# Split products with w_out for the last four steps of the first chunk: POOL rounds the blocks, VectorE makes the square

## The chip, the cores and the metric

The kernel runs on one core of a Trainium2 chip. The metric is the device time of one execution in microseconds (us), as a median of runs. The engines are TensorE (PE in the profile; its weight loads are PEld), VectorE (DVE), ScalarE (ACT), GpSimd (POOL) and SyncE (SP, which here only issues transfers). Each engine takes its instructions in the order in which the program gives them to it and waits for the others by semaphores.

## The reference

Block-sparse attention is followed by a two-layer feed-forward block:

```python
# q, k, v: (4, 8, 768, 64); blocks of 32 tokens; mask by blocks
scores = scale * q @ k.T              # where the mask allows
attn = softmax(scores)
x = (attn @ v).transpose(0, 2, 1, 3).reshape(3072, 512)
h = np.maximum(x @ w_in, 0.0)         # w_in: (512, 2048)
return (h * h @ w_out)                # w_out: (2048, 512)
```

A block of queries sees its neighbours, the first and the last block, and three sampled blocks; the first and last block of queries see everything. The weights come as 64-bit floats, the rest as 32-bit floats.

## The kernel before

**Chunks and steps.** The 3072 tokens are worked in eight chunks `c` of 384 tokens (three tiles of 128). The feed-forward block of a chunk, `moe(c)`, has 16 steps `f`, one for each 128 of the 2048 hidden units. `hidden(c, f)` makes 128 hidden units for the 384 tokens: 12 matmuls (L928), four pieces of `w_in` by three products (high x high, low x high, high x low: both `w_in` and `x` are split into a part rounded to the matmul's reduced format, `fp32r`, and a remainder). `finish` (L945) takes the result out of PSUM: relu `r` on ACT, then the square. `project(c, f)` (L965) multiplies the square by block `f` of `w_out` and adds into three PSUM banks, one for each tile of tokens. It runs `LEAD` = 2 steps behind the hidden step, so that `project(c, 14)` and `project(c, 15)` stand at the start of `moe(c + 1)`, after the last hidden step of `c` and before the first of `c + 1`.

**Two ways to project.** In chunk 0, with `PLAIN` = 16, all steps take the plain way: square `gp` in full 32 bits (L952), full `WO[f]`, three matmuls (L972), each of which the hardware runs in two passes. Later chunks take the split way: `gh` rounded by ACT (L955), `gf` in full by DVE (L960), `gl = gf - gh` by POOL (L962), and the block `w_out` as `wo`: a rounded half and a remainder, made by `split` (L887): the rounding on DVE (L892; in chunk 0 on ACT, L890), the subtraction on POOL (L893). A split step has nine matmuls (L982), `gh` by the rounded half, `gh` by the remainder, `gl` by the rounded half for each tile of tokens. The blocks `wi` of `w_in` are made by `split` in the same way, once per step, one step ahead of the hidden step that needs them.

**Unpacking the weights.** In chunk 0 the weights arrive as 64-bit words (`craw`, transfers issued by POOL) and are cut to 32 bits: two operations on ACT (L841, L843) and two on DVE (L852, L853) for a block. The order is the list `cuts`; its last entries are `w_out` 12, `w_in` 15, `w_out` 13, 14 and 15. `cut_next` moves the list on at fixed counts; `need` moves it on where a block is wanted sooner. In the kernel before no call of `need` in the last steps has anything left to do.

**The order of work.** Nothing is rearranged: each engine gets its instructions in the order in which the Python code runs (`manual_schedule`, L1043). `moe` is a generator; after each of its `yield`s a counter `now` goes on by one, and `work.step(now)` adds what the attention of a coming chunk has due then (scores, maxima, exponentials, moves of blocks, products with the values). Around the change the counts are: step 12's project from 78, step 13's from 84, `finish` of step 15 at 89, `moe(1)` from 89 on: the splits of `x` for chunk 1 (`xh` by ACT, L912; `xl` by DVE, L916), attention's maxima (L678 to L682), at 90 the split of `wi` 1, then `project(0, 14)` from 90 and `project(0, 15)` from 93, and the output of chunk 0 at 96. Two lines of `moe` matter most:

```python
            if c == 0 and f > 0:
                split_wo(c, f - 1)          # L1034, before project(c, f - 2)
...
                if c == 1 and f == NF - 1:
                    split_wo(0, f)          # L1018, before project(0, 15)
```

With `PLAIN` = 16 both calls return at once. In iteration `f` of chunk 0 the split of `wi` for step `f + 1` comes first.

**Buffers.** The tiles tagged `w` (raw blocks, `wi`, `wo`, and attention's `pg` and `pgm`) share seven buffers in turn; `gh`, `gf`, `gl` and `r` have two each. Hidden products, scores and attention's outputs share five PSUM banks, the projections have three.

Of the kernel before, what the change touches and what calls it, by code (L numbers as in the profile page):

```python
# [14 lines left out]
AF = mybir.ActivationFunctionType  # L15
ALU = mybir.AluOpType
# [33 lines left out]
TOK = UC * P  # L50
# [45 lines left out]

WO_LOW = 3
W1_LOW = 5
PLAIN = 16


def f32(ap):
# [4 lines left out]
def tile_block_sparse_attention_moe(ctx: ExitStack, tc, kd, knd, qd, qgd, vd, vnd, samp, const, wcat, out):  # L107
# [9 lines left out]
    nc = tc.nc  # L117
# [55 lines left out]
    WO = {f: one.tile([P, DM], F32, name=f"WO{f}") for f in range(WO_LOW)}  # L173
# [637 lines left out]
    wo = {}  # L811
# [3 lines left out]
    acc = {}  # L815
# [67 lines left out]
    def need(f, part):  # L883
        while done["split"] <= cuts.index((f, part)):
            cut_next()

    def split(c, src, name):  # L887
        w = rot.tile([P, 2, DM], F32R, tag="w", name=name, bufs=WBUFS)
        if c == 0:
            nc.scalar.copy(w[:, 0], src)  # L890
        else:
            nc.vector.tensor_copy(w[:, 0], src)  # L892
        nc.gpsimd.tensor_tensor(w[:, 1], src, w[:, 0], op=ALU.subtract)  # L893
        return w

    def split_wo(c, f):
        if c == 0:
            if f < PLAIN:
                return
            need(f, 1)  # L900
        wo[c, f] = split(c, WO[f], f"wo{c}_{f}")

    def parts(c, i, a, z):

# [34 lines left out]
    def hidden(c, f):  # L939
        yield from half_hidden(c, f, 2 if (c, f) in ph else 0, NCC)  # L940
        finish(c, f)
        if f < NF - 1:
            yield 0.7

    def finish(c, f):  # L945
        acc = ph.pop((c, f))
        wi1.pop((c, f), None)
        r = pool["x"].tile([P, TOK], F32, tag="r", name=f"r{c}_{f}", bufs=2)
        nc.scalar.activation(r, acc[:, :TOK], AF.Relu)  # L949
        if c == 0 and f < PLAIN:  # L950
            gt[c, f] = pool["x"].tile([P, TOK], F32, tag="gh", name=f"gp{c}_{f}", bufs=2)
            nc.scalar.activation(gt[c, f], r, AF.Square)  # L952
            return
        gh = pool["x"].tile([P, TOK], F32R, tag="gh", name=f"gh{c}_{f}", bufs=2)
        nc.scalar.activation(gh, r, AF.Square)  # L955
        gf = pool["x"].tile([P, TOK], F32, tag="gf", name=f"gf{c}_{f}", bufs=2)
        if c == 0:
            nc.scalar.activation(gf, r, AF.Square)
        else:
            nc.vector.scalar_tensor_tensor(gf, acc[:, :TOK], 0.0, r, op0=ALU.max, op1=ALU.mult)  # L960
        gl = pool["x"].tile([P, TOK], F32R, tag="gl", name=f"gl{c}_{f}", bufs=2)
        nc.gpsimd.tensor_tensor(gl, gf, gh, op=ALU.subtract)  # L962
        gt[c, f] = (gh, gl)

    def project(c, f):  # L965
        if f == 0:
            acc[c] = [ps_o.tile([P, 512], F32, tag="o", name=f"po{c}_{u}") for u in range(UC)]
        if c == 0 and f < PLAIN:
            need(f, 1)
# [36 lines left out]
    def moe(c):  # L1006
# [6 lines left out]
        if c > 0:  # L1013
            yield 0.7
            if c < NCH:
                wi1[c, 1] = split(c, W1[1], f"wi{c}_1")
            for f in range(NF - LEAD, NF):
                if c == 1 and f == NF - 1:  # L1018
                    split_wo(0, f)
                yield from project(c - 1, f)  # L1020
            emit_out(c - 1)
        if c == NCH:
            return
        for f in range(NF):
            for n in (f, f + 1) if f == 0 else (f + 1,):
                if n < NF and (c, n) not in wi1:
                    if c == 0:
                        need(n, 0)
                    if n in SINGLE:
                        wi1[c, n] = split(c, W1[n], f"wi{c}_{n}")  # L1030
            if c == 0 and f == 0:
                for n in range(2):
                    yield from half_hidden(c, n, 0, NCC // 2)
            if c == 0 and f > 0:  # L1034
                split_wo(c, f - 1)
            if f >= LEAD:
                yield from project(c, f - LEAD)
            if c > 0:
                split_wo(c, f)
            yield from hidden(c, f)  # L1040
# [64 lines left out]
    while work.todo or work.running or now < SPLIT_0[-1]:  # L1105
# [16 lines left out]
        if now in SPLIT_0:  # L1122
            f = 1 + SPLIT_0.index(now)
# [88 lines left out]
```

## Time and profile before

| what | value |
|---|---|
| time, median of 3 runs | 738.68 us (738.59 to 739.42) |
| the profiled execution's own time | 735.78 us |
| its span, first to last instruction | 733.9 us |
| L928, hidden products (960 high, 480 low) | 275.5 and 161.9 us busy |
| L972, plain projections of chunk 0 (96 passes) | 48.6 us busy |
| L982, split projections of chunks 1 to 7 (672 and 336 matmuls) | 211.7 and 134.5 us busy |
| first and last L972 | 55.1 and 151.2 us |
| granted TensorE clock, mean | 0.998 |

The times of the profile count from the first instruction. `busy` is the time in which at least one instruction of a group ran; matmuls overlap, so the start of one to the start of the next tells more than their durations. In a row of the timeline the bracket at the end is the idle time of the engine ahead of it and what ended it. In the windows each engine has its busy time and its number of instructions; behind them come the granted clock, the share of the DMA engines and GB/s.

### The profile page before, as it was taken

To read this page: it belongs to the slowest core of one execution; us is meant where nothing else is said; L and a number is where in the kernel's file an instruction comes from. 1 tells how busy PE (TensorE), PEld (TensorE's weight loads), DVE (VectorE), ACT (ScalarE), POOL (GpSimd) and SP (SyncE) were. 2 spreads that over 40 slices of the span, in tenths; PEclk is the share of its full clock that TensorE was granted. 3 is DMA by queue.
4 is the path that set the end of the run, shared out by engine and by line. 5 is a ranking of instruction groups with operands and counts; after the bars stand their busy time and mean duration, and the time that the engine had idled before them with its cause. 6 is when DMAs were issued, how large, how long until landed. Compare 5 with 4: busy or idle time off the path is not lost.

```text
span 733.9 us, 21489 instructions
## 1 busy us (share of the span) xinstructions
PE 707.5 (96%) x7496; PEld 566.3 (77%) x7496; DVE 530.1 (72%) x1058; ACT 499.7 (68%) x1116; POOL 553.6 (75%) x711
## 2 busy tenths in 40 slices
PE   5879999999999999999999999999999999999997
PEld 3555666677788888877878888887778888888996
DVE  5786888687786868679776877768877686647552
ACT  5877878988856866688775875678776767622222
POOL 8969968368766768869776587768877577868985
PEclk9999999999999999999999999999999999999999
DMA  8978897555545565554635556635455352101001
GB/s 279 228 208 264 241 355 243 146 140 148 169 124 120 168 192 155 125 133 138 186 80 137 166 155 194 152 91 153 119 146 147 97 158 49 34 1 44 1 1 43
DMA packets 91886, 105.10 MB, mean 143 GB/s; under 512 B 13667, under 2 KB 77668, under 8 KB 91780
## 3 DMA queue, kind: packets, MB, share of 16 engines
q1 hardware_dynamic: 85972, 81.15, 41.8%
q0 software_dynamic: 5664, 22.45, 9.1%
q8 instruction: 60, 0.98, 0.6%
q14 instruction: 46, 0.38, 0.2%
q10 hardware_dynamic: 144, 0.13, 0.1%
HBM read 97.39 MB, written 6.29 MB: 141 GB/s over the span
## 4 chain that ended last, share of the span: by engine, by line
PE 82%; DVE 8%; POOL 3%; issue 3%; ACT 3%; DMA 1%; POOLq 0%; DVEq 0%; ACTq 0%
PE ph L928 33%; PE po L982 27%; PE s L478 6%; PE pv L573 6%; PE po L972 5%; PE pvg L734 2%; PE g L664 2%; DVE m L490 1%; PE pt L552 1%; POOL gl L962 1%; DVE p L497 1%; DVE pT L528 1%; DVE gf L960 1%; POOL pgm L700 1%; DVE xl L916 1%
## 5 line engine op out<-in xcount | busy, mean ns | idle before, releaser
L928 PE MATMUL ph<-xh,wi 128*128 128x384 f32 x960 | 275.5, 347 | 0.0
L522 ACT ACTIVATE pm<-p 32x256 f32<-32x256 f32 x528 | 219.2, 415 | 15.2 <-DVE p L497 8.0
L982 PE MATMUL po<-wo,gh 128*128 128x512 f32 x672 | 211.7, 396 | 0.4 <-ACT gh L955 0.3
L893 POOL TENSOR_TENSOR wi<-W,wi 128x512 fp32r<-128x512 f32 x120 | 164.3, 1369 | 60.7 <-DVE wi L892 37.9
L928 PEld LDWEIGHTS ph<-xh,wi 128*128 128x128 f32 x960 | 174.2, 188 | 21.7 <-issue 12.1
L949 ACT ACTIVATE r<-ph 128x384 f32<-128x384 f32 x128 | 63.0, 492 | 173.0 <-PE ph L928 172.4
L893 POOL TENSOR_TENSOR wo<-WO,wo 128x512 fp32r<-128x512 f32 x112 | 144.7, 1292 | 34.5 <-DVE wo L892 33.1
L962 POOL TENSOR_TENSOR gl<-gf,gh 128x384 fp32r<-128x384 f32 x112 | 118.7, 1060 | 65.0 <-DVE gf L960 56.2
L928 PE MATMUL ph<-xl,wi 128*128 128x384 f32 x480 | 161.9, 337 | 0.0
L982 PEld LDWEIGHTS po<-wo,gh 128*128 128x128 f32 x672 | 123.0, 188 | 27.4 <-issue 7.5
L960 DVE SCALAR_TENSOR_TENSOR gf<-ph,r 128x384 f32<-128x384 f32 x112 | 62.0, 554 | 107.7 <-ACT r L949 99.7
L982 PE MATMUL po<-wo,gl 128*128 128x512 f32 x336 | 134.5, 400 | 4.9 <-POOL gl L962 4.8
L928 PEld LDWEIGHTS ph<-xl,wi 128*128 128x128 f32 x480 | 90.2, 188 | 9.1 <-issue 5.4
L892 DVE CAST wo<-WO 128x512 fp32r<-128x512 f32 x112 | 86.4, 772 | 0.0
L982 PEld LDWEIGHTS po<-wo,gl 128*128 128x128 f32 x336 | 63.0, 187 | 24.5 <-POOL gl L962 11.2
L955 ACT ACTIVATE gh<-r 128x384 fp32r<-128x384 f32 x112 | 58.9, 526 | 10.7 <-POOL pgm L700 0.7
L490 DVE TENSOR_REDUCE m<-s 128x2 f32<-128x512 f32 (+1 forms) x96 | 61.0, 675 | 1.6 <-PE s L478 1.5
L892 DVE CAST wi<-W 128x512 fp32r<-128x512 f32 x105 | 60.7, 578 | 0.0
L573 PEld LDWEIGHTS pv<-V,pT 128*32 128x32 f32 x2816 | 42.5, 110 | 23.0 <-issue 13.8
L573 PE MATMUL pv<-V,pT 128*32 128x65 f32 x2816 | 50.8, 222 | 4.9 <-issue 4.0
L478 PE MATMUL s<-KG,q 64*32 64x256 f32 x1408 | 52.9, 382 | 0.0
L972 PE MATMUL po<-WO,gp 128*128 128x512 f32 x96 | 48.6, 622 | 1.9 <-DVE WO L853 1.9
(93 smaller groups left out, 771.6 us busy)
## 6 DMA issues: line engine op xcount, KB each, us to landing
craw<-in_w_dram POOLq DMA_DIRECT2D x32, 512.0 KB, 5.6
V<-in_v_dram SPq DMA_DIRECT2D x462, 32.5 KB, 2.4
KG<-in_k_dram SPq DMA_DIRECT2D x189, 64.0 KB, 1.9
V<-in_v_dram SPq DMA_DIRECT2D x28, 390.0 KB, 5.3
KG<-in_k_dram SPq DMA_DIRECT2D x12, 768.0 KB, 5.8
q<-in_q_dram SPq DMA_DIRECT2D x24, 256.0 KB, 3.1
out_dram<-ot SPq DMA_DIRECT2D x23, 256.0 KB, 4.6
V<-in_v_dram SPq DMA_DIRECT2D x14, 292.5 KB, 5.0
```

What stands on the lines that cost most here:

```text
L478: nc.tensor.matmul(self.sb[e][g * BLK : (g + 1) * BLK, i * NSLOT : (i + 1) * NSLOT], q[r, j, pr, :], kg[r, j, :, pr, :], start=True, stop= ...
L490: nc.vector.tensor_reduce(m[at, e], self.sb[e][at].rearrange("p (i c) -> p i c", i=2), axis=AX, op=ALU.max)
L522: nc.scalar.activation(p[a * BLK : (a + 1) * BLK, g], x[g * BLK : (g + 1) * BLK, :, a], AF.Exp, scale=SCALE)
L573: nc.tensor.matmul(po[h * BLK : (h + 1) * BLK, g * VW : (g + 1) * VW], self.pT[:, g, 2 * e + i, c], v[:, self.u, j, h * VW : (h + 1) * VW] ...
L892: nc.vector.tensor_copy(w[:, 0], src)
L893: nc.gpsimd.tensor_tensor(w[:, 1], src, w[:, 0], op=ALU.subtract)
L928: nc.tensor.matmul(ph[c, f][:, :TOK], wi[:, w, cc], x[:, cc], start=(cc == 0 and i == 0), stop=(cc == NCC - 1 and i == 2),)
L949: nc.scalar.activation(r, acc[:, :TOK], AF.Relu)
L960: nc.vector.scalar_tensor_tensor(gf, acc[:, :TOK], 0.0, r, op0=ALU.max, op1=ALU.mult)
L962: nc.gpsimd.tensor_tensor(gl, gf, gh, op=ALU.subtract)
L972: nc.tensor.matmul(acc[c][u], g[:, u * P : (u + 1) * P], WO[f], start=(f == 0), stop=(f == NF - 1))
L982: nc.tensor.matmul(acc[c][u], g[:, at], w[:, k], start=(f == 0 and i == 0), stop=(f == NF - 1 and i == 2))
```

## The change

The constant `PLAIN` goes from 16 to 12, so steps 12 to 15 of chunk 0 take the split way. For them POOL makes the rounded half of `wo` as well as the remainder, where the code before would have used ACT, and DVE makes the full square `gf`. The rounding of `wi` stays on ACT in chunk 0.

```diff
-PLAIN = 16
+PLAIN = 12
...
-    def split(c, src, name):
+    def split(c, src, name, copy=None):
         w = rot.tile([P, 2, DM], F32R, tag="w", name=name, bufs=WBUFS)
-        if c == 0:
-            nc.scalar.copy(w[:, 0], src)
-        else:
-            nc.vector.tensor_copy(w[:, 0], src)
+        (copy or (nc.vector.tensor_copy if c else nc.scalar.copy))(w[:, 0], src)
         nc.gpsimd.tensor_tensor(w[:, 1], src, w[:, 0], op=ALU.subtract)
         return w
...
-        wo[c, f] = split(c, WO[f], f"wo{c}_{f}")
+        wo[c, f] = split(c, WO[f], f"wo{c}_{f}", None if c else nc.gpsimd.tensor_copy)
...
         gf = pool["x"].tile([P, TOK], F32, tag="gf", name=f"gf{c}_{f}", bufs=2)
-        if c == 0:
-            nc.scalar.activation(gf, r, AF.Square)
-        else:
-            nc.vector.scalar_tensor_tensor(gf, acc[:, :TOK], 0.0, r, op0=ALU.max, op1=ALU.mult)
+        nc.vector.scalar_tensor_tensor(gf, acc[:, :TOK], 0.0, r, op0=ALU.max, op1=ALU.mult)
```

## The prediction

> **What bounds the kernel now.** I read the page's head first, then the chain of waits from 126 to 160 us, then the order of work on POOL, ScalarE (ACT) and VectorE (DVE) in that stretch.
>
> ```profile
> span 733.9 us, 21489 instructions
> PE 707.5 (96%) x7496; PEld 566.3 (77%) x7496; DVE 530.1 (72%) x1058; ACT 499.7 (68%) x1116; POOL 553.6 (75%) x711
> ```
>
> TensorE is busy 96% of the span, so a change matters by what it takes from TensorE's work or adds to its waits. The steps concerned lie here (start, length, what):
>
> ```profile
> 134.00 1.72 PE po L972 x4
> ...
> 137.59 1.40 PE ph L928 x8
> ...
> 140.91 2.57 PE po L972 x6
> 143.48 1.40 PE ph L928 x8
> ...
> 145.69 0.91 PE ph L928 x4
> 146.59 5.15 PE po L972 x12
> 151.74 2.12 PE ph L928 x12
> ...
> 158.34 2.09 PE po L982 x9
> ```
>
> Every piece of this chain is a TensorE piece. L972 is the plain product with `w_out`, six passes a step: step 12 starts at 134.00, step 13 at 140.91, steps 14 and 15 run back to back from 146.59 to 151.74. L982 at 158.34 is a later chunk's step, nine passes. A plain step takes 5.15 / 2 = 2.57 us, a split step 2.09 us.
>
> **What TensorE gains.** Four steps at 2.57 - 2.09 = 0.48 us, so 1.9 us in all, 0.26% of the span. That is all there is to win, and only if the split blocks are there in time.
>
> **What the other engines get.** Nothing changes on ACT: two squares a step become one square for the product (524 ns before, 526 ns after by the same shape), and DVE makes the other. The prices of the rest, each from a row of the same shape (min/median/max ns for L859 and L860, mean ns in the group rows):
>
> ```profile
> L962 POOL TENSOR_TENSOR gl<-gf,gh 128x384 fp32r<-128x384 f32 x112 | 118.7, 1060 | 65.0 <-DVE gf L960 56.2
> L960 DVE SCALAR_TENSOR_TENSOR gf<-ph,r 128x384 f32<-128x384 f32 x112 | 62.0, 554 | 107.7 <-ACT r L949 99.7
> L955 ACT ACTIVATE gh<-r 128x384 fp32r<-128x384 f32 x112 | 58.9, 526 | 10.7 <-POOL pgm L700 0.7
> L859 POOL CAST WI<-ct x1: 746/746/746, 39.1 to 39.1; 128x512 fp32r<-128x512 f32 x1
> L860 POOL TENSOR_TENSOR WI<-ct,WI x1: 1272/1272/1272, 39.9 to 39.9; 128x512 fp32r<-128x512 f32 x1
> L952 ACT ACTIVATE gp<-r x16: 522/524/526, 53.3 to 147.2; 128x384 f32<-128x384 f32 x16
> ```
>
> DVE gets 4 x 0.55 = 2.2 us. POOL gets 4 x (0.75 + 1.27 + 1.06) = 12.3 us. L859 is the very operation that the change puts on POOL, a rounding copy of a 128x512 block. Started one behind the other, rounding and subtraction take 39.9 - 39.1 + 1.27 = 2.07 us. POOL has room for the sum; what decides is where the pieces stand in its order.
>
> ```profile
> 130.83 1.27 POOL L893 TENSOR_TENSOR wi<-W,wi 128x512 fp32r<-128x512 f32 x1 [4.95 <-ACT wi L890]
> 139.04 1.28 POOL L893 TENSOR_TENSOR wi<-W,wi 128x512 fp32r<-128x512 f32 x1 [6.94 <-ACT wi L890]
> 140.26 0.61 POOL L357 COPY KG<-kn 128x512 f32<-128x512 f32 x1
> 140.81 3.01 POOL L700 COPY pgm<-pg 32x192 f32<-32x192 f32 x8
> 152.25 1.30 POOL L893 TENSOR_TENSOR wi<-W,wi 128x512 fp32r<-128x512 f32 x1 [8.43 <-DVE wi L892]
> 153.48 0.62 POOL L357 COPY KG<-kn 128x512 f32<-128x512 f32 x1
> ```
>
> These are the `wi` splits of steps 14 and 15 and of step 1 of the next chunk, each after a long wait (bracket). In `moe`, each new `wo` split stands right behind one of them: wo12 behind wi14, wo13 behind wi15, and wo15 behind wi1 of chunk 1 (wo14 stands alone). POOL takes its instructions in order, so its idle time ahead of these rows cannot be used by the new work behind them.
>
> **wo12, no cost.** wi14 ends at 132.1, so wo12 is complete at 132.1 + 2.07 = 134.2; TensorE wants its second half one pass after 134.00, at 134.23. DVE's new square of step 12 waits for the same relu that ACT makes now. So step 12 saves its 0.48 and TensorE is through with hidden step 14 at 140.91 - 0.48 = 140.43.
>
> **wo13, a short wait.** ACT sets its start:
>
> ```profile
> 134.65 0.49 ACT L949 ACTIVATE r<-ph 128x384 f32<-128x384 f32 x1
> ...
> 138.35 0.62 ACT L890 CAST wi<-W 128x512 fp32r<-128x512 f32 x1
> ...
> 141.86 0.49 ACT L949 ACTIVATE r<-ph 128x384 f32<-128x384 f32 x1
> ...
> 146.63 0.49 ACT L949 ACTIVATE r<-ph 128x384 f32<-128x384 f32 x1 [0.69 <-PE ph L928]
> ...
> 147.58 1.64 ACT L912 CAST xh<-x 128x512 fp32r<-128x512 f32 x3
> ```
>
> The cast of wi15 starts at 138.35 in ACT's order whatever TensorE gains: the relu at 134.65 shows no wait, nor does any ACT row up to 146.63. wi15 leaves POOL at 140.32, wo13 at 140.32 + 2.07 = 142.39. TensorE stands from 140.43, does one pass at about 141.1 (first half), and goes on at 142.45: 142.45 + 8 x 0.232 = 144.31, against 143.48 before. Step 13 is late by 0.8 us net. Behind the DVE square of step 13, which waits for the relu at 134.65, lie the unpacking of the last two `w_out` blocks; they come up to 2 us later and are not wanted before wo14. Hidden step 15 takes its 3.11 us (143.48 to 146.59) and ends at 147.4 instead of 146.59.
>
> **wo14, covered.** After 142.39 POOL has the key copy (0.61), eight moves (3.01), `gl` of step 14 (1.06) and wo14 (2.07). By their place three moves come ahead of wo14: 147.2. With all eight ahead it would be 149.1. TensorE wants it at 147.4; a wait of up to 1.7 us is hidden under the next one. Step 14 then ends at 149.5.
>
> **wo15, the long wait.** It stands behind wi1 of chunk 1, and that waits for a chain that starts when hidden step 15 ends:
>
> ```profile
> 148.22 1.90 DVE L916 TENSOR_TENSOR xl<-x,xh 128x512 fp32r<-128x512 f32 x3 [4.78 <-ACT xh L912]
> 150.03 1.16 DVE L678 TENSOR_REDUCE g<-g 128x1 f32<-128x384 f32 x2
> ...
> 151.66 0.42 DVE L892 CAST wi<-W 128x512 fp32r<-128x512 f32 x1
> ```
>
> Relu at 146.63, square, three roundings of x from 147.58, their remainders on DVE to 150.1, two maxima with small operations, the cast at 151.66, POOL's wi1 at 152.25. So wi1 starts 152.25 - 146.59 = 5.66 us after hidden step 15, and POOL starts its next instruction at 153.48, 6.89 us after. In the kernel before nobody on TensorE's path waits for that: 5.15 us of plain products and then a first hidden step with another block lie over it. Now the last product does: 6.89 + 2.07 = 8.96 us after hidden step 15, so at 147.4 + 9.0 = 156.4, TensorE going on at 156.5 and ending step 15 at 156.5 + 1.86 = 158.4. Before, it ended at 151.74. That is +6.6 us with all gains and the earlier wait in it. TensorE has nothing else between: no other line stands between steps 14 and 15 in the chain, and the whole next chunk is queued behind step 15. Bounds: the rounding has one row; by the shortest conversion, the 0.42 us cast, it would be 0.3 less, by a slowed copy 0.4 more.
>
> **The clock.** The gap of before that I go by is one of 1.91 us near 53 to 55 us (columns: window, length, busy us of PE, PEld, DVE, ACT, POOL, then the granted clock):
>
> ```profile
> 34.00:36.00 2.00, 0.23 (x13) 0.23 (x12) 0.36 (x1) 0.20 (x1) 2.00 (x8) 1.00 0.74 170
> ```
> ```profile
> 52.00:54.00 2.00, 1.17 (x6) 0.85 (x6) 1.47 (x2) 1.97 (x5) 2.00 (x2) 1.00 0.37 83
> 54.00:56.00 2.00, 0.93 (x2) 0.44 (x3) 1.97 (x4) 1.97 (x5) 2.00 (x6) 0.81 0.35 67
> 56.00:58.00 2.00, 2.00 (x4) 0.91 (x3) 1.70 (x4) 1.74 (x4) 2.00 (x5) 0.50 0.74 195
> 58.00:60.00 2.00, 2.00 (x7) 1.06 (x6) 1.19 (x2) 0.00 (x0) 2.00 (x8) 0.83 0.80 187
> ```
> ```profile
> 55.07 4.51 PE L972 MATMUL po<-WO,gp 128*128 128x512 f32 x6 [1.91 <-DVE WO L853]
> ```
>
> After that gap the granted clock fell to half for a while. Lost at full clock: 2 x (0.19 + 0.50 + 0.17) = 1.7 us. The gap of up to 1.8 us in 34 to 36 left it at 1.00, so gaps under 2 us go either way. The new gap is 149.5 to 156.5, some 7 us with one pass in it, so I take the same 1.7 us behind it. Bounds: 0 if the clock is back before step 15, and 3.4 us if the low spell is twice as long.
>
> The Trainium skill ("TensorE: Matmul & The Clock Gate", Part 1) says that the clock halves only after an idle window of about 3.4 us and returns after a busy window of the same length. For wo15 this agrees with my term; the row at 55.07 disagrees, as 1.91 us of idling already sufficed there, and by the page the short wait for wo13 could not cost clock, which is what the sum takes; the row leaves it open (second rival).
>
> **What comes back.** TensorE later waits for other engines, and those have more lead after the stall. The first such place:
>
> ```profile
> 195.00:197.00 2.00, 1.55 (x9) 1.11 (x7) 1.36 (x2) 1.94 (x6) 1.81 (x4) 1.00 1.03 330
> 197.00:199.00 2.00, 1.31 (x26) 1.00 (x26) 0.00 (x0) 1.85 (x5) 2.00 (x3) 1.00 0.75 140
> ```
>
> There TensorE is idle 0.45 + 0.69 = 1.1 us. Between 0 and 1.1 us can return; I take 0.5. The buffers: the `w` ring has seven, and wo12 to wo15 take those of two raw blocks, wi13 and wo12, all used up by then: nothing.
>
> **Contention.** DVE's unpacking beside POOL's subtraction:
>
> ```profile
> 128.18 0.65 DVE L852 SCALAR_TENSOR_TENSOR W<-W,craw 128x512 int32<-128x512 int32 x1
> ...
> 131.10 1.55 DVE L852 SCALAR_TENSOR_TENSOR WO<-WO,craw 128x512 int32<-128x512 int32 x1
> ```
>
> The second ran while POOL had wi14 (130.83 to 132.1) and took 0.9 us more; POOL's 1.27 was not stretched. So the new POOL work slows DVE's unpacking by up to 0.9 us for each meeting, ahead of wo13 only, where the wait for ACT's cast covers it. I take nothing, with 0.7 us (one unpacking) for POOL as the upper bound.
>
> The Trainium skill ("SBUF — State Buffer", Who interferes with whom) calls this an exclusive lock that whoever starts first holds for the whole instruction, which would put up to one unpacking, an estimate of 0.7 us by the row at 128.18, on any new POOL piece. The row at 131.10 agrees for DVE; no row here shows POOL losing.
>
> **Sum.** +6.6 + 1.7 - 0.5 = +7.8 us. The profiled execution took 735.78 us (span 733.9 and 1.9 around it); it would be 743.6. The median of the three runs is 738.68, 2.9 us above that execution; the difference carries over, so 738.68 + 7.8 = 746.5 us.
>
> **Rivals.**
> - The clock holds or is back in time: +6.6 - 0.5 = +6.1, 744.8 us. For it: 34 to 36 us, where a gap cost nothing. Against: the 1.91 us gap did cost, and this one is over three times as long. Chance 0.20.
> - The clock falls at wo13's wait too: gaps of 0.6 and 1.1 us close together are near the 1.91 that sufficed; another 1.6 us, +9.4, 748.1 us. Chance 0.11.
> - The other side, faster: the wo15 split reaches POOL ahead of wi1, for instance because the program's POOL order isn't that of the source. POOL is through with the moves and wo14 at 149.1 and with `gl` of step 15 at 150.2; wo15 right behind would be complete at 152.3, and at 149.5 if some of these moves went behind it. With that, and wo13 ahead of wi15, all four savings stand: -1.9, 736.8 us. Against: POOL sits 8.43 us idle ahead of wi1 with a key copy behind it. It decides from the moment wo15 is ready before step 14 ends. Chance 0.05.
> - Half of that: wo15 comes early but not wo13, or the stall is taken back later as other engines run ahead; within 0.2%, about 739 us. Against: after 200 us TensorE's windows are nearly full, so there is little to take back. Chance 0.04.
>
> **The numbers.** The forecast has chance 0.60 and lies at 746.5. 0.2% is 1.5 us, about what a measurement of this kernel can tell from no change. Slower by more: 0.60 + 0.20 + 0.11 = 0.91; within: 0.04; faster: 0.05. The range takes the first rival with all 1.1 us coming back and 0.3 off the rounding (738.68 + 6.6 - 1.1 - 0.3 = 743.9), a further microsecond below for waits sized from one execution, and above the second rival with 0.7 of contention and 0.4 of copying (749.2): 743.0 to 749.2.
>
> **What would show it.** Right: a TensorE gap of 6 to 7 us between steps 14 and 15, ended by POOL's `wo` subtraction at L893's place, about 9 us after hidden step 15; in it POOL waiting for DVE's cast of `wi`; one of 1 to 2 us in step 13; a granted clock under 1.00 in the 4 us behind the long gap; L982 in 36 more matmuls, L972 in 24 fewer. Wrong: steps 14 and 15 back to back, POOL's new subtraction ahead of wi1, or the delay gone by 200 us.

## The result

Medians: 738.77 us before (735.92 to 739.49, 6 runs), 745.82 us after (743.39 to 747.27, 6 runs). They lie 7.1 us apart. The ratio is 1.0111, with a 95% interval of 1.0091 to 1.0132: slower by 8 us, between 6.7 and 9.8. In a later job the same kernel had 1.0125 (1.0107 to 1.0142). The forecast was +7.8 us.

The profiled execution took 743.39 us. In `after.py` the lines have moved: L925 is the hidden product, L966 the plain projection, L976 the split one, L889 the rounding and L890 the subtraction of a split block, L954 the full square, L956 its remainder, L909 and L913 the splits of x. The head of its page and two of its groups (busy us, mean ns, then idle time ahead):

```profile
span 741.6 us, 21541 instructions
PE 709.1 (96%) x7508; PEld 570.0 (77%) x7508; DVE 536.4 (72%) x1062; ACT 499.9 (67%) x1116; POOL 566.1 (76%) x723
...
L976 PE MATMUL po<-wo,gh 128*128 128x512 f32 x696 | 221.8, 399 | 7.9 <-POOL wo L889 6.1
...
L976 PE MATMUL po<-wo,gl 128*128 128x512 f32 x348 | 139.9, 402 | 5.0 <-POOL gl L956 4.9
```

L976 has 24 + 12 = 36 matmuls more; POOL's busy time grew by 12.5 us, DVE's by 6.3, of which the new squares are 2.3. One wait of 6.1 us for POOL stands out. TensorE's own rows of that place (start, length, line; in the bracket the idle time ahead):

```profile
147.13 0.63 PE L976 MATMUL po<-wo,gh 128*128 128x512 f32 x2
147.59 0.39 PE L976 MATMUL po<-wo,gl 128*128 128x512 f32 x1
154.07 0.80 PE L976 MATMUL po<-wo,gh 128*128 128x512 f32 x1 [6.09 <-POOL wo L889]
155.42 0.80 PE L976 MATMUL po<-wo,gh 128*128 128x512 f32 x1 [0.55 <-POOL wo L890]
...
158.57 0.63 PE L976 MATMUL po<-wo,gl 128*128 128x512 f32 x1
159.00 0.52 PE L925 MATMUL ph<-xh,WI 128*128 128x384 f32 x1
```

The first two rows are the end of step 14; step 15's first pass had to wait for the rounded half of its block, its second for the remainder. The chain of waits of the same stretch, which was TensorE alone before, now leaves TensorE:

```profile
145.94 0.50 ACT r L946
...
146.52 0.53 ACT gh L952
147.05 0.52 ACT xh L909
...
147.59 2.56 DVE xl L913 x3
...
151.78 0.34 DVE wi L889
...
152.19 1.27 POOL wi L890
153.46 0.56 POOL wo L889
...
154.09 1.28 POOL wo L890
...
155.42 3.78 PE po L976 x8
159.20 2.79 PE ph L925 x12
```

From the last hidden step of chunk 0 it runs through ACT's relu, square and roundings of x, DVE's remainders, maxima and cast of `wi` 1, and POOL's `wi` 1, to the two POOL operations that make wo15. The windows (window, length, busy us of PE, PEld, DVE, ACT, POOL, granted clock, share of the DMA engines, GB/s) show what followed:

```profile
148.00:150.00 2.00, 0.00 (x0) 0.00 (x0) 2.00 (x3) 1.94 (x6) 0.39 (x1) 1.00 0.24 52
150.00:152.00 2.00, 0.00 (x0) 0.00 (x0) 1.88 (x7) 0.85 (x3) 0.00 (x0) 0.58 0.60 163
152.00:154.00 2.00, 0.00 (x0) 0.00 (x0) 1.00 (x2) 1.76 (x4) 1.81 (x2) 0.50 0.37 104
154.00:156.00 2.00, 1.38 (x2) 0.79 (x3) 0.00 (x0) 0.00 (x0) 1.84 (x3) 0.50 0.35 100
156.00:158.00 2.00, 2.00 (x6) 1.60 (x5) 0.74 (x2) 0.00 (x0) 0.00 (x0) 0.50 0.43 120
158.00:160.00 2.00, 2.00 (x7) 1.71 (x7) 0.98 (x2) 0.69 (x2) 0.87 (x1) 0.50 0.69 80
160.00:162.00 2.00, 2.00 (x15) 1.76 (x17) 0.00 (x0) 1.08 (x3) 0.68 (x2) 0.86 0.82 258
```

The clock fell to half during the gap and came back at about 160.6 us, after step 15 and more than half of a hidden step.

**A ruler.** Executions of one kernel differ in their first 65 us, where transfers arrive: attention's scores at L664 that stood at 128.42 in the profile of before start between 126.77 and 134.60 in the others. So traces are compared by the distance from the start of those scores to the start of the last matmul ("ruler" below): 601.1 us before (128.42 to 729.52), 610.7 after (126.77 to 737.51): +9.6 us. To the first matmul of chunk 1 it is 22.8 before (151.18) and 32.2 after (159.00): +9.5. Nearly all of the loss lies there.

### The profile page after: what moved, and what is told of

Read it like the earlier page. It is cut to its first block, busy times and chain, and to the rows that moved or that the text cites. A ratio compares the mean times of both kernels' runs of the same rounds, so it can differ in the third digit from the quotient of the medians.

```text
span 741.6 us, 21541 instructions
## 1 busy us (share of the span) xinstructions
PE 709.1 (96%) x7508; PEld 570.0 (77%) x7508; DVE 536.4 (72%) x1062; ACT 499.9 (67%) x1116; POOL 566.1 (76%) x723
## 4 chain that ended last, share of the span: by engine, by line
PE 78%; DVE 9%; ACT 5%; POOL 4%; issue 2%; DMA 2%; POOLq 0%; DVEq 0%; ACTq 0%
PE ph L925 32%; PE po L976 28%; PE pv L573 6%; PE s L478 6%; PE po L966 3%; PE pvg L734 2%; PE g L664 1%; DVE m L490 1%; DMA kn<-in_kn_dram 1%; DVE xl L913 1%; POOL gl L956 1%; DVE p L497 1%; DVE pT L528 1%; POOL wo L890 1%; ACT r L946 1%
## 5 line engine op out<-in xcount | busy, mean ns | idle before, releaser
L925 PE MATMUL ph<-xh,wi 128*128 128x384 f32 x960 | 274.8, 346 | 0.0
L976 PE MATMUL po<-wo,gh 128*128 128x512 f32 x696 | 221.8, 399 | 7.9 <-POOL wo L889 6.1
L890 POOL TENSOR_TENSOR wi<-W,wi 128x512 fp32r<-128x512 f32 x120 | 163.9, 1366 | 46.8 <-DVE wi L889 33.3
L925 PEld LDWEIGHTS ph<-xh,wi 128*128 128x128 f32 x960 | 174.3, 188 | 21.6 <-issue 12.0
L890 POOL TENSOR_TENSOR wo<-WO,wo 128x512 fp32r<-128x512 f32 x116 | 150.0, 1293 | 38.4 <-DVE wo L889 35.9
L956 POOL TENSOR_TENSOR gl<-gf,gh 128x384 fp32r<-128x384 f32 x116 | 123.6, 1065 | 71.8 <-DVE gf L954 60.3
L925 PE MATMUL ph<-xl,wi 128*128 128x384 f32 x480 | 161.9, 337 | 0.0
L976 PEld LDWEIGHTS po<-wo,gh 128*128 128x128 f32 x696 | 128.2, 189 | 37.8 <-issue 7.5
L954 DVE SCALAR_TENSOR_TENSOR gf<-ph,r 128x384 f32<-128x384 f32 x116 | 64.3, 554 | 115.6 <-ACT r L946 106.2
L976 PE MATMUL po<-wo,gl 128*128 128x512 f32 x348 | 139.9, 402 | 5.0 <-POOL gl L956 4.9
L925 PEld LDWEIGHTS ph<-xl,wi 128*128 128x128 f32 x480 | 90.1, 188 | 8.8 <-issue 5.0
L889 DVE CAST wo<-WO 128x512 fp32r<-128x512 f32 x112 | 85.8, 766 | 0.0
L976 PEld LDWEIGHTS po<-wo,gl 128*128 128x128 f32 x348 | 65.7, 189 | 25.1 <-POOL gl L956 11.3
L952 ACT ACTIVATE gh<-r 128x384 fp32r<-128x384 f32 x116 | 61.0, 526 | 10.4
L889 DVE CAST wi<-W 128x512 fp32r<-128x512 f32 x105 | 61.4, 585 | 0.0
L497 DVE TENSOR_TENSOR p<-s,m 128x512 f32<-128x512 f32 (+1 forms) x72 | 45.9, 676 | 0.0
```

Of the source, the lines that this page charges most:

```text
L889: (copy or (nc.vector.tensor_copy if c else nc.scalar.copy))(w[:, 0], src)
L925: nc.tensor.matmul(ph[c, f][:, :TOK], wi[:, w, cc], x[:, cc], start=(cc == 0 and i == 0), stop=(cc == NCC - 1 and i == 2),)
L976: nc.tensor.matmul(acc[c][u], g[:, at], w[:, k], start=(f == 0 and i == 0), stop=(f == NF - 1 and i == 2))
```

## The experiments

The theory: wo15 stands on POOL behind `wi` 1 of chunk 1, and that waits for x of the next chunk; the idle time halves the clock; wo13 adds a small wait. Rival 1: POOL's 12 us of new work slow the stretch, wherever they stand. Rival 2: the loss is spread over the four steps. Rival 3: the clock costs nothing. The ratios stand against the kernel before in the same job; the ruler is read from one trace of each kernel.

| kernel | ratio, 95% interval | ruler, us | ruler to chunk 1, us |
|---|---|---|---|
| before | 1 | 601.1 | 22.8 |
| the change | 1.0111 (1.0091 to 1.0132) | 610.7 | 32.2 |
| the change again | 1.0125 (1.0107 to 1.0142) | 610.4 | 32.3 |
| only step 15 split | 1.0123 (1.0100 to 1.0147) | 609.2 | 31.1 |
| steps 12 to 14 split | 1.0019 (1.0002 to 1.0036) | 602.1 | 23.2 |
| wo15 ahead of `wi` 1 | 1.0059 (1.0036 to 1.0083) | 606.6 | 27.9 |
| `wi` 1 ahead of x | 1.0096 (1.0072 to 1.0120) | 607.9 | 29.6 |
| wo15 behind wo14 | 1.0064 (1.0041 to 1.0087) | 606.0 | 27.8 |
| wo13 and wo15 early | 1.0038 (1.0014 to 1.0061) | 606.3 | 27.1 |
| the same, `gl` 15 on DVE | 1.0001 (0.9986 to 1.0016) | 601.6 | 22.3 |
| 12 to 14 split, wo13 early | 1.0004 (0.9986 to 1.0021) | 601.8 | 22.4 |
| gap filled in part | 1.0093 (1.0057 to 1.0129) | 609.9 | 32.2 |
| gap filled | 1.0107 (1.0086 to 1.0127) | 608.6 | 30.6 |
| gap filled, again | 1.0080 (1.0064 to 1.0096) | 609.3 | 31.1 |

### Which step costs

Two kernels replace `f < PLAIN` by a tuple of the split steps:

```diff
-PLAIN = 12
+SPLIT_0_WO = (15,)          # the other kernel: (12, 13, 14)
```

Only step 15:

> Only step 15 is split, steps 12 to 14 plain. Theory: wo15 is complete about 9 us after hidden step 15 as in the change (there 155.4 - 145.9 = 9.5), step 15 then takes 1.9 to 3.8 us, against 5.15 us from hidden step 15 to the end of step 15 before; with the low clock also in the first hidden step: +6 to +8.5 us, nearly the whole of the change's loss. Rival (the loss is spread over the four steps): about a quarter, +2 us.

Steps 12 to 14:

> Steps 12 to 14 split as in the change, step 15 plain. Theory (the loss is step 15's block behind wi 1, and the clock after it): no long gap and no low clock; step 13's wait puts hidden step 15 1.0 us late and step 14 saves 0.48, so 0 to +1 us against before, in the trace from the scores near 128 us to the last matmul too. Rival (the new work of POOL as such slows the stretch): +3 us or more.

One step of the four gave nearly all of the change's loss: +9.1 us in time by its ratio (1.0123 of 736.0), a little over what was expected, and +8.0 by the ruler. The other three together gave +1.4 and +1.0. Rival 2 falls, and so does rival 1 as it stands: the kernel with three new blocks on POOL is slower by at most 2.6 us. TensorE in the kernel with step 15 alone split, where step 14 is plain:

```profile
148.41 2.74 PE L966 MATMUL po<-WO,gp 128*128 128x512 f32 x6
156.60 0.80 PE L976 MATMUL po<-wo,gh 128*128 128x512 f32 x1 [5.46 <-POOL wo L889]
157.95 0.79 PE L976 MATMUL po<-wo,gh 128*128 128x512 f32 x1 [0.55 <-POOL wo L890]
```

Step 15's second pass comes 157.95 - 148.41 = 9.5 us after the first matmul of step 14, which follows hidden step 15 at once; in the change it is 155.42 - 145.74 = 9.7.

### What wo15 waits for

The place on POOL, with the rest as in the change:

```diff
+            if c == 1:
+                split_wo(0, NF - 1)
             if c < NCH:
                 wi1[c, 1] = split(c, W1[1], f"wi{c}_1")
             for f in range(NF - LEAD, NF):
-                if c == 1 and f == NF - 1:
-                    split_wo(0, f)
```

> wo15 goes to POOL ahead of the split of wi 1 of chunk 1, still after gl of step 15. Theory (wo15 stands behind a block that waits for x of the next chunk): in the changed kernel's trace gl 15 leaves POOL at 148.4, so wo15 is complete at 150.4 instead of 155.4; TensorE ends step 15 at about 152.3, 2.2 us later than the kernel before at the same place, with 0 to 1.7 us for the clock: 2 to 4 us slower than before. Rival 1 (POOL simply has too much work): as slow as the change, 7 to 8 us over before. Rival 2 (the late result is due to the clock alone): also near the change, as a gap stays.

And the wait itself, with the order `wi` 1, wo15 kept, but `wi` 1 cast before x:

```diff
+        if c == 1:
+            wi1[c, 1] = split(c, W1[1], f"wi{c}_1")
         if 0 < c < NCH:
             for i in range(UC):
                 high(c, i, 0, NCC, nc.scalar.copy)
                 low(c, i, 0, NCC)
...
-            if c < NCH:
+            if 1 < c < NCH:
                 wi1[c, 1] = split(c, W1[1], f"wi{c}_1")
```

> The split of wi 1 of chunk 1 stands ahead of the roundings and remainders of x for chunk 1, and still ahead of wo15 on POOL. Theory (it isn't the place behind wi 1 but DVE's late cast, which waits for x, that costs): on the changed kernel's clock POOL does wi1 at 148.4, wo15 from 149.7 to 151.7, some more if x's remainders contend; step 15 goes on 3 to 3.7 us sooner than in the change: +4 to +6 against before. Rival (POOL's order alone): as the change, +8 to +9.6.

By the ruler to chunk 1 the first is 4.3 us below the change, the second 2.6; both sit between the kernel before and the change, as the theory has it and the rivals don't. In time only the first is clear of the change; the second's interval overlaps the change's, so it rests on its trace. Both missed their expected size on the slow side (+5.5 and +6.8 by the ruler). The cause is seen in the second kernel's POOL and DVE:

```profile
155.01 1.71 POOL L890 TENSOR_TENSOR wi<-W,wi 128x512 fp32r<-128x512 f32 x1
156.68 1.07 POOL L889 CAST wo<-WO 128x512 fp32r<-128x512 f32 x1
157.82 1.58 POOL L890 TENSOR_TENSOR wo<-WO,wo 128x512 fp32r<-128x512 f32 x1
```
```profile
154.22 4.07 DVE L913 TENSOR_TENSOR xl<-x,xh 128x512 fp32r<-128x512 f32 x3
```

Beside the remainders of x POOL's rounding took 1.07 us instead of 0.61 and its subtractions 1.58 to 1.71 instead of 1.27; the remainders took 4.07 us for three, 1.90 in the kernel before. The first kernel shows the same: 1.07 and 1.59 us on POOL, 4.02 on DVE. In the second kernel gaps of 3.2 and 1.2 us were left, in the first 1.5 and 1.2, and the clock fell in them too.

### Getting the block in time

```diff
             if c == 0 and f > 0:
                 split_wo(c, f - 1)
+                if f == NF - 1:
+                    split_wo(c, f)
```

> wo15 goes to POOL right behind wo14, in iteration 15 of chunk 0. Theory: no long gap, no low clock; step 13's wait stays. Hidden step 15 ends 1.0 us later than before (as in the changed kernel), steps 14 and 15 then save 0.96: 0 us against before, between -0.5 and +0.7. Rival (POOL's 12 us of new work is the cost): still over +3 us.

The second kernel does this and also puts these lines ahead of the `wi` split of the same iteration:

> In chunk 0 each wo split stands ahead of the wi split of the same iteration, and wo15 right behind wo14. Theory: all four savings, 1.9 us, less what ACT's order takes back: relu 15 follows ACT's other work at about 145.0 on the changed kernel's clock, the remainders of x end at about 149.4, against 150.1 at which the kernel before started chunk 1: between -0.7 and -1.9 us. Rival (a split step costs POOL and DVE as much as it saves TensorE): 0 or slower.

Both missed: +0.64% and +0.38% instead of none and a gain. The wait for wo15 was gone, but another had taken its place. In the second kernel, TensorE and then POOL:

```profile
150.88 0.61 PE L976 MATMUL po<-wo,gh 128*128 128x512 f32 x2
154.96 0.50 PE L976 MATMUL po<-wo,gl 128*128 128x512 f32 x1 [3.46 <-POOL gl L956]
```
```profile
148.82 0.61 POOL L889 CAST wo<-WO 128x512 fp32r<-128x512 f32 x1
149.51 1.30 POOL L890 TENSOR_TENSOR wo<-WO,wo 128x512 fp32r<-128x512 f32 x1
150.87 2.96 POOL L700 COPY pgm<-pg 32x192 f32<-32x192 f32 x5
153.91 0.99 POOL L956 TENSOR_TENSOR gl<-gf,gh 128x384 fp32r<-128x384 f32 x1
```

wo15 was ready at 150.8; but five of attention's moves, slowed to 2.96 us beside the remainders of x, and then `gl` of step 15 stood behind it, and step 15's third pass needs `gl`. The kernel with wo15 alone early waits in the same way, 3.06 us for `gl` of step 15. Here rival 1 holds in part: POOL's order has no room for wo14, wo15, the moves and `gl` 15 ahead of step 15. The proof is to take that one operation away:

```diff
-        nc.gpsimd.tensor_tensor(gl, gf, gh, op=ALU.subtract)
+        (nc.vector if (c, f) == (0, NF - 1) else nc.gpsimd).tensor_tensor(gl, gf, gh, op=ALU.subtract)
```

> The kernel with wo13 and wo15 early, and gl of step 15 made by DVE instead of POOL. Theory (there POOL's five moves and gl 15 came behind wo15, and TensorE waited 3.46 us for gl 15): that wait goes, the next in line are the remainders of x, which ended at 152.85 where the first hidden step of chunk 1 could have started at 152.8: 0 to +1 us against before, 600.5 to 602.5 us from the scores to the last matmul. Rival (wo15 itself or the new work at large is late): over +3.

The wait went (ratio 1.0001, ruler 601.6), the clock stayed at 1.00, and the next in line was the one expected:

```profile
152.64 0.34 PE L925 MATMUL ph<-xh,WI 128*128 128x384 f32 x1
153.17 0.45 PE L925 MATMUL ph<-xl,WI 128*128 128x384 f32 x1 [0.19 <-DVE xl L913]
```

Chunk 1 cannot go on sooner, as the remainders of x end there. Of the 1.9 us that four split steps save, a wait of 0.72 us for wo14 takes a part, 0.4 us arrive at chunk 1's start (22.3 against 22.8), and by the end of the ruler none.

Without step 15, and with wo13 early:

> Steps 12 to 14 split, step 15 plain, and each wo split ahead of the wi split of its iteration, so that wo13 no longer waits for ACT's cast of wi15. Theory: step 13's wait of 1.0 us goes; three savings of 0.48, less short waits for wo14 and for attention as in the kernel with both blocks early (0.57 and 0.53): -1.4 to 0 us against before. Rival (the remainders of x hold chunk 1's start anyway, as ACT's relu 15 does not come sooner): 0 to +1.

1.0004 (0.9986 to 1.0021), and 0.7 us longer by the ruler: the expected gain did not come. The number is the rival's, but its reason isn't seen: the remainders of x end at 150.57, before chunk 1 starts at 151.06, and TensorE doesn't wait for them. The wait for wo13 is gone (step 13's nine passes run without a gap), 0.79 us for wo14 came up, and 0.3 us reached chunk 1. It was lost again at the end of chunk 1, where TensorE waits 1.08 us for a `gl` at which it waited 0.21 before; why that wait grew stays open. No version here beats the kernel before by what can be measured.

### The clock

Plain matmuls into an unread bank, to keep TensorE busy in the gap; they add work and leave nothing out:

```diff
                 if c == 1 and f == NF - 1:
                     split_wo(0, f)
+                    idle = bank("idle")
+                    for _ in range(6):
+                        nc.tensor.matmul(idle, ident, WO[0], start=True, stop=True)
```

> The changed kernel with six more plain matmuls (12 passes, 5.15 us at full clock) between the projects of steps 14 and 15, into a bank that nobody reads. Theory with a clock term: the wait for wo15 ends when it did, but TensorE keeps its clock, so the low spell behind it (2.6 us in the changed kernel's trace: 3.78 instead of 1.86 for eight matmuls, 2.79 instead of 2.12 for the hidden step) goes: 2 to 3 us faster than the change, 5 to 6 over before. Rival (the clock costs nothing there, or the lost time comes back later anyway): as the change within 0.7 us.

This told nothing: its interval (1.0057 to 1.0129) spans the change. The matmuls ended early and left two gaps, and the clock fell after all:

```profile
156.43 0.50 PE L976 MATMUL po<-wo,gh 128*128 128x512 f32 x1 [0.95 <-POOL wo L889]
157.77 0.78 PE L976 MATMUL po<-wo,gh 128*128 128x512 f32 x1 [0.84 <-POOL wo L890]
```
```profile
156.00:158.00 2.00, 0.73 (x2) 0.41 (x3) 0.00 (x0) 0.15 (x1) 1.92 (x3) 0.96 0.29 82
158.00:160.00 2.00, 2.00 (x5) 1.57 (x6) 0.69 (x1) 0.00 (x0) 0.27 (x1) 0.50 0.40 115
```

The next has seven in the gap and one more behind step 15's first pass:

> The changed kernel with seven plain matmuls (6.0 us) between steps 14 and 15 and one more (0.86) behind the first pass of step 15, into a bank that nobody reads, so that no gap over 0.5 us is left. Theory with a clock term: the granted clock stays at 1.00, step 15's last eight passes take 1.9 us instead of 3.8: 2 to 3 us less than the change from the scores near 128 us to the last matmul (610.7 - 2.5 = 608). Rival (no clock cost): 610 to 611.

Its clock was 1.00 throughout. From step 15's second pass to the next chunk's first attention product it took 4.17 us (156.22 to 160.39), the change 6.49 (155.42 to 161.91): 2.3 us for the clock. The ruler fell by 2.1 us; the times, from different jobs, can't tell (1.0107 and 1.0111). So it was run again beside the change:

> The change once more, for comparison on the same chip with the kernel without gaps: 609 to 611 us from the scores to the last matmul, +7 to +9 us in time.

> The change with its gaps filled by plain matmuls once more, on the same chip as the change: theory with a clock term 2 us less than the change in time and in the trace (608 to 609 us from the scores to the last matmul, clock 1.00); rival: no difference.

```profile
154.00:156.00 2.00, 1.91 (x5) 0.57 (x3) 0.92 (x2) 1.68 (x4) 1.83 (x2) 1.00 0.41 119
156.00:158.00 2.00, 2.00 (x6) 1.04 (x7) 0.00 (x0) 0.00 (x0) 1.82 (x2) 1.00 0.35 95
158.00:160.00 2.00, 2.00 (x11) 1.74 (x10) 1.72 (x3) 0.44 (x1) 0.01 (x1) 1.00 0.40 111
```

1.0080 (1.0064 to 1.0096) beside 1.0125 (1.0107 to 1.0142) on one chip: filling the gap with useless work made the kernel faster by about 0.45%, 3.3 us in time and 1.1 by the ruler (step 15's second pass came 0.5 us later after the scores than in the change beside it). From that pass to the attention product it took 4.17 us again (157.35 to 161.52), the change beside it 6.20 (156.24 to 162.44). Both expectations were met but for a little: the change lay 9.2 us above the kernel before in time, the filled kernel at 609.3 us by the ruler. Rival 3 falls; the size lies between 1 and 3 us, with 2.0 and 2.3 read directly from the passes.

## Why the prediction was right

- **ACT, nothing.** Right (499.7 us busy before, 499.9 after), though not because two squares became one: a plain step had one square on ACT, and a split step here has one.
- **wo12, no cost.** Right but for 0.17 us of waiting: POOL's subtraction took 1.60 us instead of 1.27 beside DVE's unpacking.
- **wo13, a short wait set by ACT's cast.** Right: hidden step 15 ended 145.94 - 126.77 = 19.17 us after the scores, before 146.59 - 128.42 = 18.17: late by 1.0, predicted 0.8. Putting wo13 ahead of wi15 removed the wait.
- **wo14, covered.** Right: POOL had it at 145.4, TensorE asked at 145.74, and three moves stood ahead of it.
- **wo15, the long wait.** The mechanism was right, and shown by taking it apart. The block came 9.5 us after hidden step 15 instead of 9.0. The term that was too small is the remainders of x: 2.56 us instead of 1.90, because `gl` of step 15, new on POOL, ran beside the first of them: that one took 1.35 us, the other two 0.68 each, and with step 15 plain and no such `gl` all three took 0.69. The rounding was cheaper than its row, 0.61 instead of 0.75.
- **The clock.** It fell as in the row near 55 us; 2.3 us instead of 1.7. The low spell began in the gap, at about 150.3 by the window at 150, and ended at 160.6. In the change's second trace it began at 153.9, still in the gap, and ended at 160.7: half clock while TensorE has nothing to do costs nothing.
- **What comes back.** This step failed: nothing did. The wait of 1.14 us for `gl` in chunk 1 is there in the change too, with the same length:

```profile
205.94 0.50 PE L976 MATMUL po<-wo,gl 128*128 128x512 f32 x1 [1.14 <-POOL gl L956]
```

 Its chain starts anew with a relu that waits for TensorE, so a delay of TensorE delays all of it, and lead that other engines gained earlier is of no use.
- **Contention.** "No row here shows POOL losing" held for the rows shown, not for the whole trace of before: at 51.8 us there POOL's subtraction took 1.75 us instead of 1.27 beside DVE's unpacking. Beside the remainders of x it loses 0.3 to 0.5 us a piece. In the kernel with `wi` 1 ahead of x the two engines take turns: each of the three remainders ends about 0.55 us after POOL's instruction ahead of it, at 155.60, 157.27 and 158.29 after 155.05, 156.72 and 157.75. That agrees with the Trainium skill ("SBUF — State Buffer", SBUF: two separate sides), by which whoever starts first holds the shared ports for a whole instruction. In the change it cost about 0.7 us, in DVE's remainders.
- **The faster rival** gave all savings if wo15 came early. With wo15 early the savings did not come: `gl` 15 behind it, and then the remainders of x, were late next. The prediction saw that some of the moves would go behind wo15, but not that `gl` 15, behind them, and the remainders of x would then be what TensorE waits for.

The sum by the ruler was +9.6, in time 8 (6.7 to 9.8); the forecast of 7.8 lies in this interval. That it came so near is in part luck. In the traces all three terms of the sum were short. Step 15 ended 159.20 - 126.77 = 32.4 us after the scores, before 151.74 - 128.42 = 23.3; without the 1.9 us that the low clock cost in its last eight passes that is +7.2 instead of +6.6. The clock took 2.0 to 2.6 instead of 1.7, and nothing came back instead of 0.5.

## What to carry to other kernels

When work moves to an engine with idle time, read what ends the idle time ahead of its place in that engine's order: a slot behind an instruction that waits for the next stage is as late as that stage, however idle the engine is. Ask in the same way what then stands behind the moved work, since it may be wanted at the same moment. And price a gap on TensorE as its length plus the low clock after it, which came here after every window of the clock in which TensorE was busy for less than 1.5 of 3.41 us (below).

## What the runs showed that was not expected

- Whether a gap halves the clock depends on where it lies, and not on its length alone. The prediction's window from 34 to 36 us holds one gap of 2.02 us (33.8 to 35.8), longer than the 1.91 us that cost the clock later, and it cost nothing. In each trace of this case the granted clock changes only at moments that lie whole multiples of 3.41 us apart. Cut into such windows, the traces show:

| trace | window, us | TensorE busy, us | clock in the next window |
|---|---|---|---|
| before | 31.36 to 34.77 | 2.39 | 1.00 |
| before | 34.77 to 38.18 | 2.41 | 1.00 |
| before | 51.84 to 55.25 | 1.50 | 0.50 |
| the change | 146.92 to 150.34 | 1.06 | 0.50 |
| the change again | 147.07 to 150.48 | 1.73 | 1.00 |
| the change again | 150.48 to 153.89 | 0.00 | 0.50 |
| gap filled in part | 154.41 to 157.82 | 1.62 | 0.50 |

  The edge at 34.77 us splits the gap of 2.02 us over two windows, each of which stays busy enough; the gap of 1.91 us lies in one. In the partly filled kernel the gaps of 0.95 and 0.84 us lie in one window. Over all 14 traces each of the 28 windows at full clock with less than 1.5 us of busy time was followed by half clock, and none of the nearly 2900 with more than 2.1 us; in between both occur (busy times are the profile's, in which the ends of matmuls are modelled). The Trainium skill ("TensorE: Matmul & The Clock Gate", Part 1) names an idle window of about 3.4 us. The length agrees, and the low spell from 150.3 to 160.6 us is three such windows long; but a window need not be wholly idle, as these rows show.
- The unread matmuls are an odd case of more work in less time: eight more products, and 0.45% faster than the change.
